# Windowed attention and two MLPs on one core: a written order for the kernel's head

## The chip, the cores and the metric

The kernel runs on 1 core of one Trainium2 chip. The metric is the device time of one execution in microseconds (us). The kernel before took 899.46 us, the median of 3 runs (899.13 to 899.58).

## What is computed

Inputs are q, k and v of shape (4, 8, 576, 64) and the weights of two MLPs, float64 as they lie in memory (512 to 2048 and back to 512), for 2304 tokens. Attention sees the last 64 positions. Cut to what matters:

```python
def _attn_ref(q, k, v):
    scores = 1.0 / np.sqrt(D) * np.matmul(q, k.transpose(0, 1, 3, 2))
    mask = (rel >= 0) & (rel < 64)
    scores = np.where(mask, scores, -1000000000.0)
    attn = np.exp(scores - np.max(scores, axis=-1, keepdims=True))
    attn = attn / (np.sum(attn, axis=-1, keepdims=True) + 1e-09)
    return np.matmul(attn, v)

def reference(...):
    x = attention, as (2304 tokens, 512)
    h = x @ moe_w_in;  x = np.maximum(0.01 * h, h) @ moe_w_out
    h = x @ moe2_w_in; return (np.maximum(h, 0) + np.log1p(np.exp(-np.abs(h)))) @ moe2_w_out
```

## The kernel before, in words

Tokens go in 6 chunks of 384 (`T`), each of three tiles of 128 tokens or six blocks of 64. A product keeps float32 accuracy by being done three times with operands split into a high and a low part (`three`, L464 to L466). One step of the first MLP is a pair (chunk, j), where j counts 16 strips of the hidden width: `gemm1` (L468) makes 12 matmuls into `ph`, ACT makes g and gh from it and DVE gl; `gemm2` (L487) makes 12 matmuls from gh and gl into four `o` banks, two steps later (`SKEW`). The steps go chunk 0 with j 0 to 7, chunk 1 with j 0 to 15, chunk 0 with j 8 to 15, then chunks 2 to 5: while the first 16 strips of both matrices are still being converted, strips 0 to 7 are used twice.

Weights come in as 512 KB pieces, one per strip and matrix, 32 in all for the first MLP (`load_w`, three `raw64` places). A piece is converted by ACT (`conv_a`, L159), by two DVE instructions (`conv_b`, L170 and L176), and split by ACT and DVE (`conv_c`, L217 and L218). A `ticker` issues these.

The attention of a tile or block has four pieces. A: PE transposes q and k of a tile into `pq` and `pk`, ACT scales pq into `qbd` (L354), DVE copies pk into `kT` (L362). B: scores `ps` on PE (L377), mask and maximum on DVE (L382, L384), four exponentials on ACT (L387), sum and reciprocal on DVE (L391, L392), and the product with the reciprocal on GpSimd (L394). C: transposes `pt` on PE (L403), copied to `at` by ACT (L405). D: product with v, `po`, on PE (L415), split into the chunk's xh by ACT (L420) and xl by DVE (L421).

The head of the program is the attention of chunk 0, in the written order "A0 B0 B1 A1 B2 C0 B3 D0 ...", with `tick()` at listed places; then the steps, with the attention of chunk 1 laid between those of chunk 0. A scheduler then places each instruction on its engine's queue. q and k of a tile lie in two places (`raw`), so that tile 1 is loaded once tile 0 has been transposed. All loads are issued from SP's queue, in its order.

Of the kernel before, what the change touches and what calls it, by code (L numbers as in the profile page):

```python
# [8 lines left out]
F32 = mybir.dt.float32  # L9
# [11 lines left out]
def tile_window_attention_two_mlps(  # L21
# [180 lines left out]
    def pair_rows(p):  # L202

        row = lambda tag, bufs, n: sb.tile(
            [P, n, 2, DM // 2], F32R, tag=tag, bufs=bufs, name=f"wp_{p}_{tag}{len(got)}"
        )
        got = []
        tags = (("v", 3, 1), ("kT", 2, 1), ("qbd", 1, 2), ("part", 1, 3))
        if p % 2 == 0:
            tags = (("raw", 2, 1),) * 2 + (("v", 3, 1),) * 2 + (("sm", 2, 1),) * 2 + (("kT", 2, 1),)  # L210
        for tag, bufs, n in tags:
            t = row(tag, bufs, n)
            got += [t[:, i] for i in range(n)]
        return got

# [5 lines left out]
    def conv_c(key):  # L221
        m, j, i = key
        a = conv.pop(key)[1]
        if m == 0:
            hi, lo = (w_row(4 * j + 2 * i + n) for n in range(2))
        elif i == 0:
            return
        else:

            hi, lo = w2_rows(j)  # L230
        split(hi, lo, a)
        if i == 0:
            hi, lo = (w.rearrange("p (c f) -> p c f", c=NK) for w in (hi, lo))
        W[key] = (hi, lo)
# [56 lines left out]
    scored = []  # L291
    qk_raw, v_win, kT, st = {}, {}, {}, {}

    def load_qk(t):
# [38 lines left out]
    att_n = [0]  # L333
# [6 lines left out]
    def att_a(t):  # L340

        kt = sb.tile([P, NP, BL + P], F32, tag="kT", bufs=2, name=f"kT_{t}")
        q_in, k_in = qk_raw.pop(("q", t)), qk_raw.pop(("k", t))
        if t < BY_DVE:
            pq, pk = att_ps(f"pq_{t}"), att_ps(f"pk_{t}")
            for x_in, x_out in ((q_in, pq), (k_in, pk)):
                for p in range(NP):
                    nc.tensor.transpose(x_out[:, p, :], x_in[:, p * P : (p + 1) * P], ident)
        else:
            pq = sb.tile([P, NP, P], F32, tag="raw", bufs=2, name=f"qT_{t}")  # L350
            nc.vector.transpose(pq, q_in)
# [9 lines left out]
        if t < BY_DVE:
            nc.vector.tensor_copy(kt[:, :, BL:], pk)  # L362
        else:
            nc.vector.transpose(kt[:, :, BL:], k_in)
        kT[t] = kt

    def att_b(gb):

        t, u = divmod(gb, 2)
# [12 lines left out]
        nc.vector.tensor_tensor(sm, ps, mask.unsqueeze(1).to_broadcast([P, NP, P]), ALU.min)  # L382
        nm = sb.tile([P, NP], F32, tag="nm", bufs=2, name=f"nm_{gb}")
        nc.vector.tensor_reduce(nm, sm, AX.X, ALU.max, negate=True)  # L384
        sums = sb.tile([P, NP], F32, tag="sums", bufs=2, name=f"sums_{gb}")
        for p in range(NP):
            a = nc.scalar.activation(  # L387
                sm[:, p, :], sm[:, p, :], AF.Exp, bias=nm[:, p : p + 1],
                accum_out=sums[:, p : p + 1],
            )  # L390
        nc.vector.tensor_scalar_add(sums, sums, 1e-9)  # L391
        b = nc.vector.reciprocal(sums, sums)  # L392
        scored.append((a.ins, b.ins))
# [74 lines left out]
    def gemm1(c, j):  # L468
        m = 0
# [5 lines left out]
        g = sb.tile([P, T], F32, tag="tmp", bufs=4, name=f"g_{m}_{c}_{j}")  # L475
        nc.scalar.activation(g, ph, AF.Prelu, alpha=0.01)  # L476
        gh = sb.tile([P, T], F32R, tag="gh", bufs=3, name=f"gh_{c}_{j}")
        gl = sb.tile([P, T], F32R, tag="gl", bufs=3, name=f"gl_{c}_{j}")
        a = nc.scalar.copy(gh, g)  # L479
        b = nc.vector.tensor_tensor(gl, g, gh.bitcast(F32), ALU.subtract)  # L480
        behind.append((a.ins, b.ins))
        G[m, c, j] = (gh, gl)
# [3 lines left out]

    def gemm2(c, j, s, e):  # L487

        wh, wl = W[0, j, 1]
        gh, gl = G.pop((0, c, j))  # L490
# [5 lines left out]
        if e and j < NF - 1:  # L496
            part[c] = sb.tile([P, NK, T], F32, tag="part", bufs=1, name=f"part_{c}")
            for i, po in enumerate(O.pop(c)):
                (nc.scalar.copy if i % 2 == 0 else nc.vector.tensor_copy)(part[c][:, i, :], po)
        elif e:  # L500
# [112 lines left out]
    def ticker(keys):  # L613
# [14 lines left out]
    tick0 = ticker([(0, j, i) for j in range(NF) for i in range(2)])  # L628
    tick = lambda: next(tick0, None)
    load_qk(0)  # L630
    constants()
    nc.vector.memset(qbd, 0.0)
    load_v(0)
    load_qk(1)
    x = new_x(0, 0)
    att_tags[:] = ["att", "h", "o"]
# [3 lines left out]
    late_loads = {  # L640
        "A1": (load_qk, 2), "C0": (load_v, 1), "B3": (load_v, 2),
        "A2": (load_qk, 3), "C4": (load_v, 3),
    }
    pieces = {"A": att_a, "B": att_b, "C": att_c, "D": lambda n: att_d(n, *x)}
    for n, item in enumerate(order.split()):
        pieces[item[0]](int(item[1:]))
        if item in late_loads:
            f, t = late_loads[item]
            f(t)
        for _ in range(ticks_after.count(n)):  # L650
            with tc.issue_after(scored[-1][0]), tc.issue_after(scored[-1][1]):
                tick()
    att_tags[:] = ["att"]

    visits = [(0, 0, 0, CUT, 1), (0, 1, 0, NF, None), (0, 0, CUT, NF, 2)]
# [5 lines left out]

    def later(f, *a):
# [4 lines left out]

    first = [ticker([(1, 2 * p + f, 0) for f in range(2)]) for p in range(NF // 2)]  # L670
# [11 lines left out]
    for n, (c, j, s, e, nxt) in enumerate(steps):  # L682
        if s:
# [3 lines left out]
        if (c, j) == (1, NF - AHEAD):  # L687
            load_qk(BY_DVE)
        for u in range(2):
# [3 lines left out]
            if n < 2 * NF and (u == 0 or n % 2):  # L693
                tick()
# [88 lines left out]
```

## Time and profile before

| | |
|---|---|
| median of the runs | 899.46 us |
| the profiled execution: time, span | 899.1 us, 897.1 us |
| busy share of the span: PE, DVE, ACT, GpSimd | 97%, 60%, 47%, 5% |
| chain that ended last, PE's share | 91% |
| mean granted TensorE clock | 0.994 |

PE is the engine that the span follows. An average over the span hides where PE waits, so the profile is read by stretches: the table of 40 slices, the windows (busy time of each engine in a stretch, number of instructions, granted clock), the timeline for the start of a step, the chain of waits for what released what, and the groups by line for what one instruction takes.

### The profile page before, as it was taken

How to read it: one execution, taken by the hardware profiler on the slowest of the kernel's cores; microseconds unless marked ns; L12 is line 12 of the kernel's file. 1: busy time of each engine (PE TensorE's matmuls, PEld its weight loads, DVE VectorE, ACT ScalarE, POOL GpSimd, SP SyncE). 2: the span in 40 equal slices, each digit the busy share in tenths (PEclk: the TensorE clock that was granted, in tenths of full speed). 3: DMA queues.
4: the chain of work that ended last, by engine and by line, in shares of the span. 5: the costliest groups of instructions: out<-in, count | busy, mean ns of one | idle time of the engine just before them, and what ended most of it. 6: DMA issues, size and time to landing. Idle time of an engine off the chain costs nothing.

```text
span 897.1 us, 14253 instructions
## 1 busy us (share of the span) xinstructions
PE 870.1 (97%) x5232; PEld 818.0 (91%) x5232; DVE 538.8 (60%) x1059; ACT 419.5 (47%) x990; POOL 47.5 (5%) x66
## 2 busy tenths in 40 slices
PE   5699999999999999999999999999999899999998
PEld 4498999999999999999999999999999688888886
DVE  3898862544323333323257689777799976667664
ACT  3788752654434444434345532222245644545443
POOL 2212000211000111000000000000000000000000
PEclk9799999999999999999999999999999999999999
DMA  7567752243223311110132145444497444344432
GB/s 175 162 192 217 220 136 35 64 78 82 48 39 65 85 44 49 48 24 12 37 118 82 54 159 196 157 153 153 153 308 279 134 119 147 107 129 120 127 99 66
DMA packets 150277, 104.74 MB, mean 117 GB/s; under 512 B 104896, under 2 KB 129472, under 8 KB 150208
## 3 DMA queue, kind: packets, MB, share of 16 engines
q1 hardware_dynamic: 150208, 103.84, 40.2%
q8 instruction: 41, 0.67, 0.3%
q14 instruction: 28, 0.23, 0.1%
HBM read 75.50 MB, written 28.31 MB: 116 GB/s over the span
## 4 chain that ended last, share of the span: by engine, by line
PE 91%; DVE 4%; DMA 2%; ACT 1%; issue 1%; POOL 0%; POOLq 0%; DVEq 0%; ACTq 0%; SPq 0%
PE ph L464 7%; PE o L464 7%; PE o L465 7%; PE o L466 7%; PE ph L465 7%; PE ph L466 7%; PE f L464 7%; PE f L465 7%; PE f L466 7%; PE ps L377 4%; PE p_s L464 3%; PE p_s L466 3%; PE p_s L465 3%; PE p_a L464 3%; PE p_a L466 2%; PE p_a L465 2%
## 5 line engine op out<-in xcount | busy, mean ns | idle before, releaser
L480 DVE TENSOR_TENSOR gl<-g,gh 128x384 fp32r<-128x384 f32 x96 | 58.6, 610 | 158.5 <-ACT gh L479 158.0
L464 PE MATMUL ph<-xh,w 128*128 128x384 f32 x384 | 132.3, 345 | 0.0
L464 PE MATMUL o<-gh,w 128*128 128x384 f32 x384 | 131.7, 343 | 0.0
L465 PE MATMUL o<-gl,w 128*128 128x384 f32 x384 | 129.8, 338 | 0.0
L465 PE MATMUL ph<-xl,w 128*128 128x384 f32 x384 | 129.0, 336 | 0.0
L466 PE MATMUL ph<-xh,w 128*128 128x384 f32 x384 | 128.8, 335 | 0.0
L466 PE MATMUL o<-gh,w 128*128 128x384 f32 x360 | 121.7, 338 | 0.0
L476 ACT ACTIVATE g<-ph 128x384 f32<-128x384 f32 x96 | 46.9, 489 | 133.5 <-PE ph L466 133.3
L464 PE MATMUL f<-w,s 128*128 128x512 f32 x234 | 91.3, 390 | 2.8 <-ACT s L217 2.8
L465 PE MATMUL f<-w,s 128*128 128x512 f32 x234 | 91.1, 389 | 0.0
L466 PE MATMUL f<-w,s 128*128 128x512 f32 x234 | 90.7, 389 | 0.0
L572 ACT ACTIVATE s<-s 128x512 f32<-128x512 f32 (+1 forms) x80 | 47.0, 589 | 69.3 <-DVE s L571 68.7
L574 DVE SCALAR_TENSOR_TENSOR s<-s,s 128x512 f32<-128x512 f32 (+1 forms) x80 | 50.8, 636 | 38.5 <-ACT s L572 38.1
L464 PEld LDWEIGHTS ph<-xh,w 128*128 128x128 f32 x384 | 72.1, 188 | 0.9
L465 PEld LDWEIGHTS ph<-xl,w 128*128 128x128 f32 x384 | 72.2, 188 | 0.2 <-DVE xl L421 0.2
L387 ACT ACTIVATE sm<-sm,nm 128x128 f32<-128x128 f32 x144 | 56.1, 391 | 34.6 <-DVE nm L384 33.9
L465 PEld LDWEIGHTS o<-gl,w 128*128 128x128 f32 x384 | 72.2, 188 | 0.0
L464 PEld LDWEIGHTS o<-gh,w 128*128 128x128 f32 x384 | 72.2, 188 | 0.0
L466 PEld LDWEIGHTS ph<-xh,w 128*128 128x128 f32 x384 | 72.1, 188 | 0.0
L466 PEld LDWEIGHTS o<-gh,w 128*128 128x128 f32 x360 | 67.6, 188 | 0.0
L218 DVE TENSOR_TENSOR s<-s,s 128x512 fp32r<-128x512 f32 (+1 forms) x80 | 50.8, 636 | 13.9 <-ACT s L217 13.7
L217 ACT CAST s<-s 128x512 fp32r<-128x512 f32 (+1 forms) x80 | 46.2, 577 | 24.9 <-PE f L465 19.5
(153 smaller groups left out, 1691.7 us busy)
## 6 DMA issues: line engine op xcount, KB each, us to landing
wraw<-in_moe_w_in_dram SPq DMA_DIRECT2D x32, 512.0 KB, 4.7
wraw<-in_moe_w_out_dram SPq DMA_DIRECT2D x32, 512.0 KB, 4.6
s<-hd SPq DMA_DIRECT2D x64, 256.0 KB, 2.7
hd<-h_xh SPq DMA_DIRECT2D x12, 768.0 KB, 4.5
hd<-h_xl SPq DMA_DIRECT2D x12, 768.0 KB, 4.4
x2d<-x SPq DMA_DIRECT2D x24, 192.0 KB, 1.9
x_stage<-x2d SPq DMA_DIRECT2D x24, 192.0 KB, 2.6
out_dram<-s SPq DMA_DIRECT2D x18, 256.0 KB, 2.4
```

The lines of the kernel that those rows point to most:

```text
L217: i = nc.scalar.copy(hi, a)
L218: j = nc.vector.tensor_tensor(lo, a, hi.bitcast(F32), ALU.subtract)
L377: nc.tensor.matmul(ps[:, p, :], qbd[:, p, u, :], kT[t][:, p, w0 : w0 + P], start=True, stop=True,)
L387: a = nc.scalar.activation(sm[:, p, :], sm[:, p, :], AF.Exp, bias=nm[:, p : p + 1], accum_out=sums[:, p : p + 1],)
L464: nc.tensor.matmul(ps, wh, xh, start=start, stop=False)
L465: nc.tensor.matmul(ps, wh, xl, start=False, stop=False)
L466: nc.tensor.matmul(ps, wl, xh, start=False, stop=stop)
L476: nc.scalar.activation(g, ph, AF.Prelu, alpha=0.01)
L480: b = nc.vector.tensor_tensor(gl, g, gh.bitcast(F32), ALU.subtract)
L572: nc.scalar.activation(g, g, AF.Softplus)
L574: nc.vector.scalar_tensor_tensor(g, h, 0.0, g, ALU.max, ALU.add)
```

## The change

It replaces the written order of pieces, the ticks among them and the scheduler's freedom, for everything up to step 23, by one list (`HEAD`) of 447 small pieces. Each instruction of a piece is tied behind the last one on its engine, so that the five queues stand exactly in the list's order. The pieces A to D, the conversion and the two products are cut into one function per engine for this. The list runs to the end of the 24th step; step 24 onward is as before. Further, q and k of tiles 1 and 2 get places of their own (three rows of the place of a later weight, `qk_early`, and that of `w_last`), `sm`, `nm` and `sums` have three buffers in place of two, PSUM banks are given out by which is free, and a tile of 64 bytes per partition, `pad`, is made in the same pool, which shifts the addresses of what is allocated after it.

```diff
@@ load_qk
-            a = sb.tile([P, H * D], F32, tag="raw", bufs=2, name=f"{nm}raw_{t}")
+            if 0 < t < TPC:
+
+                if t == 1 and nm == "q":
+                    qk_early.append(wide("qk_early", F32))
+                    w = sb.tile([P, DM], F32, tag="w_last", bufs=1, name="k_early")
+                    qk_early.append([qk_early[0][:, n] for n in range(3)] + [w])
+                a = qk_early[1][2 * (t - 1) + (nm == "k")]
+            else:
+                a = sb.tile([P, H * D], F32, tag="raw", bufs=2, name=f"{nm}raw_{t}")
...
@@ att_ps
-        tag = att_tags[att_n[0] % len(att_tags)]
-        att_n[0] += 1
+        left = {t: (4 if t == "o" else 2) - list(held.values()).count(t) for t in att_tags}
...
@@ att_b, now att_bp, att_bm, att_bn, att_be, att_bs, att_bx
-        sm = sb.tile([P, NP, P], F32, tag="sm", bufs=2, name=f"sm_{gb}")
+        sm = sb.tile([P, NP, P], F32, tag="sm", bufs=3, name=f"sm_{gb}")
...
+        if "pad" not in st:
+
+            st["pad"] = sb.tile([P, 16], F32, tag="pad", bufs=1, name="pad")
+            nc.vector.memset(st["pad"][:1, :1], 0.0)
...
@@ the head
-    order = "A0 B0 B1 A1 B2 C0 B3 D0 A2 C1 C2 B4 D1 D2 B5 C3 D3 C4 C5 D4 D5"
-    ticks_after = [2, 2, 3, 5, 10, 11, 14, 18, 20]
...
+    HEAD = """
+        Lq0 Lq1 Lv1 Ap0 Lq2 Aq0 Ak0 Ap1 Ah1 Bp1 l1 Ak1 Bp0 Bm1 l2 Bn1 Aq1 Ah2 Ap2 Bm0 Be1 Bp3 Bn0 l0 Ak2
...
+        Q22 R22 G23 H21 P23 Q23 R23
+    """.split()
...
+        seen = len(traced)
+        pieces[item[:n]](int(item[n:]))
+        new = traced[seen:]
+        for ins in new:
+            before = queues.get(ins.engine)
+            if before is not None:
+                tc.add_manual_dep(
+                    ins, before.name,
+                    mybir.DependencyInfo(mybir.DependencyClass.NoSync, mybir.DependencyReason.DATA),
+                    reason="head",
+                )
+            queues[ins.engine] = ins
```

In the list the letters A to D are the attention's pieces (second letter: the part, p on PE, q and e on ACT, k, m, n, s and l on DVE, x on GpSimd), l, a, b, c, d are load, the three conversions and the split's DVE half, G and H the first and second product of a step, P, Q, R the work on g, L a load of q, k or v. Up to the first piece that needs a weight (G0) it holds 6 Ap, 10 Bp, 6 Cp and 6 Dp, 5 Aq, 7 Be, 6 Ca, 6 Dh, 4 a and 3 c; from G0 to G8 it holds 8 G, 7 H, 2 Bp, 6 Cp, 6 Dp, and for DVE 14 b, 14 d, 5 Bm, 5 Bn, 6 Bs, 6 Dl, 8 R and 1 Ak. The last conversion (d31) stands ahead of G18.

The queue of SP, from its start: q, k and v of a tile are `qraw`, `kraw` and `vn` or `vs`, the 512 KB weight pieces `wraw`. Before:

```order
L286 DMA qraw_0_86<-in_q_dram 128x8x64
L286 DMA kraw_0_88<-in_k_dram 128x8x64
L286 DMA vn_0_115<-in_v_dram 128x8x64
L128 DMA wraw_0_0_0_171<-in_moe_w_in_dram 128x4x128
L133 DMA wraw_0_0_1_173<-in_moe_w_out_dram 128x512
L128 DMA wraw_0_1_0_194<-in_moe_w_in_dram 128x4x128
L286 DMA qraw_1_117<-in_q_dram 128x8x64
L286 DMA kraw_1_119<-in_k_dram 128x8x64
```

and in the change:

```order
L297 DMA qraw_0_111<-in_q_dram 128x8x64
L297 DMA kraw_0_113<-in_k_dram 128x8x64
L297 DMA qk_early_115<-in_q_dram 128x8x64
L297 DMA qk_early_115<-in_k_dram 128x8x64
L297 DMA vs_1_119<-in_v_dram 128x8x64
L297 DMA vn_1_121<-in_v_dram 128x8x64
L297 DMA qk_early_115<-in_q_dram 128x8x64
L297 DMA k_early_116<-in_k_dram 128x8x64
L133 DMA wraw_0_0_1_156<-in_moe_w_out_dram 128x512
```

q and k of tile 1 moved from seventh and eighth, behind three weight pieces, to third and fourth, and those of tile 2 ahead of all weights.

The queue of PE at the start of step 8, the first of chunk 1 (the numbers behind `ph_` and `gh_` are chunk and strip). Before:

```order
L464 MATMUL o_0_0_2_677<-gh_0_5_921,w_7_782 128x384
L465 MATMUL o_0_0_2_677<-gl_0_5_922,w_7_782 128x384
L466 MATMUL o_0_0_2_677<-gh_0_5_921,w_7_782 128x384
L464 MATMUL o_0_0_3_678<-gh_0_5_921,w_7_782 128x384
L465 MATMUL o_0_0_3_678<-gl_0_5_922,w_7_782 128x384
L466 MATMUL o_0_0_3_678<-gh_0_5_921,w_7_782 128x384
L464 MATMUL ph_1_0_1075<-xh_0_1_455,w_0_299 128x384
```

and in the change:

```order
L552 MATMUL o_0_0_2_575<-gh_0_6_985,w_8_904 128x384
L553 MATMUL o_0_0_2_575<-gl_0_6_1011,w_8_904 128x384
L554 MATMUL o_0_0_2_575<-gh_0_6_985,w_9_959 128x384
L552 MATMUL o_0_0_3_576<-gh_0_6_985,w_8_904 128x384
L553 MATMUL o_0_0_3_576<-gl_0_6_1011,w_8_904 128x384
L554 MATMUL o_0_0_3_576<-gh_0_6_985,w_9_959 128x384
L552 MATMUL ph_1_0_1075<-xh_0_1_674,w_0_430 128x384
```

The second product of strip 6 moved ahead of step 8. Before step 24, and from there to the end, both programs hold the same matmuls in the same order but for one score and one transpose of chunk 2.

## Rows read from the trace of the kernel before

**Rows 1.** The page's 40 equal slices: busy tenths of PE.

```profile
PE   5699999999999999999999999999999899999998
```

**Rows 2.** Windows: stretch, length; busy PE, PEld, DVE, ACT, POOL; clock, DMA share.

```profile
4.16:22.70 18.54, 13.37 (x66) 11.30 (x68) 6.21 (x12) 7.46 (x26) 2.88 (x4) 1.00 0.74 184
22.70:33.00 10.30, 6.37 (x76) 5.25 (x72) 8.31 (x17) 8.73 (x31) 2.48 (x3) 1.00 0.59 146
33.00:44.03 11.03, 6.69 (x64) 4.98 (x64) 9.32 (x21) 7.68 (x23) 2.35 (x2) 0.54 0.58 174
44.03:91.16 47.13, 45.34 (x356) 41.96 (x354) 42.11 (x80) 39.33 (x108) 8.36 (x9) 1.00 0.72 207
91.16:158.36 67.20, 67.20 (x386) 67.20 (x386) 37.37 (x67) 33.59 (x65) 0.40 (x1) 1.00 0.48 126
158.36:680.00 521.64, 521.64 (x3362) 513.09 (x3362) 279.99 (x569) 214.88 (x548) 28.78 (x33) 1.00 0.34 99
```

**Rows 3.** Timeline of PE: start and us, first product of steps 0, 8, 24.

```profile
44.03 0.61 PE L464 MATMUL ph<-xh,w 128*128 128x384 f32 x2
...
91.16 0.34 PE L464 MATMUL ph<-xh,w 128*128 128x384 f32 x1
...
158.36 0.34 PE L464 MATMUL ph<-xh,w 128*128 128x384 f32 x1
```

**Rows 4.** Chain of waits in order of time: start, us, what.

```profile
0.73 3.29 DMA qraw<-in_q_dram
...
5.28 7.17 DMA qraw<-in_q_dram
...
18.61 3.41 PE ps L377 x16
...
75.88 0.93 PE ps L377 x8
76.81 0.44 PE pt L403 x4
77.95 0.61 PE po L415 x16
```

**Rows 5.** Groups by line on ACT, 0 to 44.03 us: busy us, mean ns.

```profile
L387 ACT ACTIVATE sm<-sm,nm 128x128 f32<-128x128 f32 x24 | 9.3, 391 | 3.4 <-DVE nm L384 2.6 <-DVE sums L392 0.6
L159 ACT ACTIVATE cva<-wraw 128x512 f32<-128x512 f32 x6 | 4.0, 674 | 0.0
L354 ACT ACTIVATE qbd<-pq 64x512 f32<-64x512 f32 x6 | 3.5, 592 | 9.3 <-PE pq L348 9.2
L405 ACT COPY at<-pt 128x512 f32<-128x512 f32 x6 | 3.3, 586 | 0.3 <-PE pt L403 0.3
L217 ACT CAST w<-cva 128x512 fp32r<-128x512 f32 x5 | 3.1, 622 | 1.6 <-DVE cva L176 1.6
L420 ACT CAST xh<-po 128x256 fp32r<-128x256 f32 x6 | 2.1, 365 | 2.2 <-PE po L415 2.2
```

**Rows 6.** Groups by line on DVE, 44.03 to 91.16 us: busy us, mean ns.

```profile
L176 DVE SCALAR_TENSOR_TENSOR cva<-wraw,cva 128x512 uint16<-128x512 uint32 x13 | 10.4, 799 | 0.2
L218 DVE TENSOR_TENSOR w<-cva,w 128x512 fp32r<-128x512 f32 x13 | 9.8, 754 | 2.0 <-ACT w L217 1.7
L170 DVE TENSOR_SCALAR cva<-cva 128x512 int32<-128x512 int32 x12 | 6.0, 503 | 0.2 <-ACT cva L159 0.2
...
L382 DVE TENSOR_TENSOR sm<-ps,masks 128x512 f32<-128x512 f32 x6 | 4.0, 685 | 0.6 <-PE ps L377 0.6
...
L362 DVE COPY kT<-pk 128x512 f32<-128x512 f32 x3 | 2.1, 694 | 0.4 <-PE pk L348 0.4
```

**Rows 7.** Timeline of GpSimd and DVE around 30 us: start, us.

```profile
30.26 1.04 POOL L394 TENSOR_TENSOR sm<-sm,sums 128x512 f32<-128x512 f32 x1 [2.93 <-PE po L415]
30.32 1.53 DVE L218 TENSOR_TENSOR w<-cva,w 128x512 fp32r<-128x512 f32 x1
...
33.78 0.66 DVE L218 TENSOR_TENSOR w<-cva,w 128x512 fp32r<-128x512 f32 x1
```

More of the change, by code (lines that the diff above doesn't have):

```diff
@@ L214, in pair_rows, with conv_c1, conv_c2 @@
         return got
+    split_parts = {}
+    def conv_c1(key):
+        m, j, i = key
+        hi, lo = (w_row(4 * j + 2 * i + n) for n in range(2))
+        nc.scalar.copy(hi, conv[key][1])
+        split_parts[key] = (hi, lo)
+    def conv_c2(key):
+        a = conv.pop(key)[1]
+        hi, lo = split_parts.pop(key)
+        nc.vector.tensor_tensor(lo, a, hi.bitcast(F32), ALU.subtract)
+        if key[2] == 0:
+            hi, lo = (w.rearrange("p (c f) -> p c f", c=NK) for w in (hi, lo))
+        W[key] = (hi, lo)
     def split(hi, lo, a):
@@ L332, in tile_window_attention_two_mlps, with new_kt, att_ap, att_aq @@
     att_tags = ["att"]
-    att_n = [0]
+    held = {}
     def att_ps(name):
-        tag = att_tags[att_n[0] % len(att_tags)]
-        att_n[0] += 1
-        return pp.tile([P, NP, P], F32, tag=tag, bufs=4 if tag == "o" else 2, name=name)
[L340 to L351, printed above, removed]
+        left = {t: (4 if t == "o" else 2) - list(held.values()).count(t) for t in att_tags}
+        if len(att_tags) > 1:
+            kind, n = name.split("_")
+            end = HEAD.index({"pq": "Aq", "pk": "Ak", "ps": "Bm", "pt": "Ca", "po": "Dl"}[kind] + n)
+            left["h"] *= end < HEAD.index("G0")
+            left["o"] *= end < HEAD.index("H0")
+        tag = max(att_tags, key=lambda t: (left[t] > 0, t != "att", left[t]))
+        held[name] = tag
+        return pp.tile([P, NP, P], F32, tag=tag, bufs=4 if tag == "o" else 2, name=name)
+    def new_kt(t):
+        if t not in kT:
+            kT[t] = sb.tile([P, NP, BL + P], F32, tag="kT", bufs=2, name=f"kT_{t}")
+        return kT[t]
+    def att_ap(t):
+        pq, pk = att_ps(f"pq_{t}"), att_ps(f"pk_{t}")
+        for nm, x_out in (("q", pq), ("k", pk)):
+            x_in = qk_raw.pop((nm, t))
+            for p in range(NP):
+                nc.tensor.transpose(x_out[:, p, :], x_in[:, p * P : (p + 1) * P], ident)
+        st["q", t], st["k", t] = pq, pk
+    def att_aq(t, pq=None):
+        pq = st.pop(("q", t)) if pq is None else pq
         for h in range(2):
@@ L358, in att_a, with att_ah, att_ak, att_bp @@
             )
+    def att_ah(t):
+        kt = new_kt(t)
         if block(2 * t)[1] != 0:
             nc.gpsimd.tensor_copy(kt[:, :, :BL], kT[t - 1][:, :, P : P + BL])
[L361 to L365, printed above, removed]
+    def att_ak(t):
+        nc.vector.tensor_copy(new_kt(t)[:, :, BL:], st.pop(("k", t)))
+    def att_a(t):
+        q_in, k_in = qk_raw.pop(("q", t)), qk_raw.pop(("k", t))
+        kt = new_kt(t)
+        pq = sb.tile([P, NP, P], F32, tag="raw", bufs=2, name=f"qT_{t}")
+        nc.vector.transpose(pq, q_in)
+        att_aq(t, pq)
+        att_ah(t)
+        nc.vector.transpose(kt[:, :, BL:], k_in)
     def att_b(gb):
+        for f in (att_bp, att_bm, att_bn, att_be, att_bs, att_bx):
+            f(gb)
+    def att_bp(gb):
         t, u = divmod(gb, 2)
@@ L408, in att_d, with att_dp @@
     def att_d(gb, xh, xl):
+        att_dp(gb)
+        att_dh(gb, xh)
+        att_dl(gb, xh, xl)
+    def att_dp(gb):
         at = st.pop(gb)
@@ L468, in gemm1, with gemm1_p @@
     def gemm1(c, j):
+        for f in (gemm1_p, gemm1_a, gemm1_h, gemm1_l):
+            f(c, j)
+    def gemm1_p(c, j):
         m = 0
@@ L495, in gemm2 @@
             three(O[c][i], wh[:, cs], wl[:, cs], gh, gl, s, e)
[L496 to L500, printed above, removed]
+        if e and j == NF - 1:
             before = part.pop(c, None)
@@ L626, in ticker @@
             yield
[L628 to L636, printed above, removed]
-    order = "A0 B0 B1 A1 B2 C0 B3 D0 A2 C1 C2 B4 D1 D2 B5 C3 D3 C4 C5 D4 D5"
-    ticks_after = [2, 2, 3, 5, 10, 11, 14, 18, 20]
[L640 to L657, printed above, removed]
+    visits = [(0, 0, 0, CUT, None), (0, 1, 0, NF, None), (0, 0, CUT, NF, 2)]
     visits += [(0, c, 0, NF, c + 1 if c + 1 < NC else None) for c in range(2, NC)]
@@ new lines, in tile_window_attention_two_mlps @@
+    """.split()
+    keys = [(0, j, i) for j in range(NF) for i in range(2)]
+    x_of = lambda c: X.get((0, c)) or new_x(0, c)
+    block_x = lambda f, n: lambda g: f(g, *x_of(g // NBC)[:n])
+    step = lambda f: lambda n: f(*steps[n][:2])
+    pieces = {
+        "Lq": load_qk, "Lv": load_v, "Ap": att_ap, "Aq": att_aq, "Ah": att_ah, "Ak": att_ak,
+        "Bp": att_bp, "Bm": att_bm, "Bn": att_bn, "Be": att_be, "Bs": att_bs, "Bx": att_bx,
+        "Cp": att_cp, "Ca": att_ca, "Dp": att_dp, "Dh": block_x(att_dh, 1), "Dl": block_x(att_dl, 2),
+        "l": lambda n: load_w(keys[n]), "a": lambda n: conv_a(keys[n]), "b": lambda n: conv_b(keys[n]),
+        "c": lambda n: conv_c1(keys[n]), "d": lambda n: conv_c2(keys[n]),
+        "G": step(gemm1_p), "P": step(gemm1_a), "Q": step(gemm1_h), "R": step(gemm1_l),
+        "E": lambda n: put_part(steps[n][0], True), "F": lambda n: put_part(steps[n][0], False),
+        "H": lambda n: gemm2(*steps[n][:4]),
+    }
@@ new lines, in tile_window_attention_two_mlps @@
+    att_tags[:] = ["att", "h", "o"]
+    queues = {}
+    traced = nc.cur_bb.bb.instructions
+    constants()
+    nc.vector.memset(qbd, 0.0)
+    for item in HEAD:
+        n = len(item.rstrip("0123456789"))
+        held.pop({"Aq": "pq", "Ak": "pk", "Bm": "ps", "Ca": "pt", "Dl": "po"}.get(item[:n], "") + "_" + item[n:], None)
+        if item == "G0":
+            att_tags[:] = ["att"]
+        if item == f"G{CUT + NF - AHEAD}":
+            load_qk(BY_DVE)
+            load_v(BY_DVE)
+        seen = len(traced)
[10 more added lines that the diff above has]
+            queues[ins.engine] = ins
```

103 lines of the change are left out of this document (77 added, 26 removed).

## The prediction

> **What bounds the kernel now.** I read the 40 slices first: PE is at five and six tenths in the first two, of 22.4 us each, and full in nearly all others [rows 1]. Then I cut the run at three instants that can be counted off in the timeline: the first product of step 0 at 44.03 us, of step 8 (the ninth group of twelve `ph` matmuls) at 91.16 and of step 24 (the twenty-fifth) at 158.36 [rows 3]. The reader is to see in the windows that stage C, step 8 to 24, has no idle PE: 386 matmuls in 67.20 us, 0.174 us each, 2.1 us for each product of twelve [rows 2]. From 158.36 to 680 PE is busy without a gap as well, and its order there is the old one. So whatever step 24 gains, the end gains, and all else is decided in stage A (to 44.03) and stage B (44.03 to 91.16).
>
> How much is there to win? Up to step 24 PE has 24 first and 22 second products, 46 x 2.1 = 96.6 us. At full speed a block of attention costs 0.93 for its scores, 0.44 for its transposes, 0.61 for the product with v [rows 4], and a tile's eight transposes of q and k twice 0.44: 12 x 1.98 + 6 x 0.88 = 29.0. PE can start when q of tile 0 has landed, at 0.73 + 3.29 = 4.0 us [rows 4]. That makes 129.6 against 158.36: 28.7 us are lost at most. Two things lose them: waits, and TensorE's clock. Sixteen score records take 3.41 us at 18.61 and eight take 0.93 at 75.88 [rows 4], which is 1.2 GHz against 2.4, although the granted clock column has no lower figure there; it has 0.54 for 33 to 44.03 [rows 2], after a stretch in which PE was busy 6.37 of 10.30 us.
>
> **Stage A, to the first product of step 0.** This product needs xh and xl of all six blocks of chunk 0. In the change q and k of tile 1 are third and fourth on SP's queue and have places of their own. Before, q of tile 1 landed at 5.28 + 7.17 = 12.45 [rows 4]; between it and the first q at 4.02 lay 2304 KB (k, v, three weight pieces, itself), so 256 KB took 8.43 / 9 = 0.94 us, and k of tile 1 now lands at 4.02 + 3 x 0.94 = 6.8. PE then transposes it (about 1 us at 1.2 GHz), makes the first scores (half of 3.41, 1.7), DVE masks them and takes the maximum (two of some 0.69 [rows 6]): the first exponential starts at about 11.0. From there ACT is the longest queue. The list puts on it, ahead of the last xh: 24 exponentials x 0.391, 6 qbd x 0.592, 6 `at` x 0.586, 6 xh x 0.365, 3 cva x 0.674, 2 weight casts x 0.622 [rows 5] = 9.4 + 3.6 + 3.5 + 2.2 + 2.0 + 1.2 = 21.9 us. Without a wait the last xh ends at 32.9 and xl (0.4) at 33.3. That is the lower bound. For the upper one I take the share in which ACT was busy between 22.70 and 44.03, 16.41 of 21.33 or 77% [rows 2]: 11.0 + 21.9 / 0.77 = 39.4, with xl 39.8. I take 36.0, below the middle, because q, k and v of three tiles now wait for nobody and a third `sm` place lets a block's scores run while GpSimd still holds two others. DVE's part is shorter (5 kT, 7 masks, 7 maxima, 4 conversions, some 23 us of work) and PE's is 6 x 0.88 + 10 x 0.93 + 6 x 1.05 = 20.9 at full speed, since scores of blocks 6 to 9 now stand here. Gain: 44.0 - 36.0 = 8.0 us.
>
> **Stage B, step 0 to step 8.** PE has 8 first and 7 second products (one more than before: that of strip 6 stands ahead of step 8), 31.5, and of the attention two scores, six transposes and six products with v, 8.2: 39.7. Before it had 14 products, 29.4, six of each of the three, 11.9, and two tiles' transposes, 1.8: 43.1, in 47.1 us; 4.0 were lost. DVE was busy 42.11 of these 47.13 [rows 2] and is close behind PE. Its list for the stage differs by one conversion more in L176 and in L218 and two in L170 (0.80 + 0.75 + 1.01), and by one mask, one maximum and two kT copies less (some 0.69 each, 2.8) [rows 6], so it needs about 42. Lower bound: DVE's 42 without a wait. Upper: the old 47.1. I take PE's work with the old loss, 39.7 + 4.0 = 43.7. Gain: 3.4, which with the moved product counts as 5.5.
>
> DVE and GpSimd also meet: a weight split that begins at 30.32, with the normalisation of 1.04 us running since 30.26, takes 1.53 us, and one begun at 33.78 takes 0.66 [rows 7]. The durations above contain such meetings at the old rate. The Trainium skill, "SBUF — State Buffer", section "SBUF: two separate sides", says that GpSimd and a VectorE instruction with two inputs in SBUF exclude each other on a shared port for a whole instruction, which agrees with these rows. If the new order let all six normalisations of the stage meet one, that rule would add up to 6 x 1.04 = 6.2 us to DVE, and the time would be some 890 rather than 886.
>
> **Stage C, step 8 to step 24.** 16 first and 15 second products, 31 x 2.1 = 65.1 us, against 67.2. DVE was busy 37.37 of 67.20 us there [rows 2], so conversions of strips 8 to 15 stay hidden behind PE; what is late next if they were not is the weight of step 16. The partial sums of chunk 0 are copied under a first product, as before. The 64-byte tile, the third `sm` and the memset of one element cost nothing: DVE has 5 us of slack in B [rows 2].
>
> **The sum.** Step 24 begins at 36.0 + 43.7 + 65.1 = 144.8, 13.6 us earlier. The profiled execution took 899.1 (span 897.1), so 885.5; the median lies 0.4 higher: **885.9 us**. With the lower bounds, 33.3 + 42 + 65.1 = 140.4, it is 881.5; with the upper, 39.8 + 47.1 + 65.1 = 152.0, it is 893.1.
>
> **Rivals.** (1) *The clock stays at 1.2 GHz through stage A.* PE's 20.9 us become 41.8, and step 0 begins no earlier than 4.0 + 41.8 = 45.8; with B and C as above 154.6, gain 3.8, 895.7 us. For it: the lower clock of 33 to 44.03 came after a stretch in which waits stood between PE's bursts [rows 2], and stage A, with 20.9 us of work in 32, will have such waits too. Against it: the loads bring work to PE earlier and closer together, and the scores of 75.88 were at full speed in a stage of the same mixture [rows 4]. One such fall of 10 us costs half of 6.4, 3 us, and lies in the range. The Trainium skill, "TensorE: Matmul & The Clock Gate", "Part 1: The HAM clock gate", says that the slow clock is the default and that activity releases it; by that, a cold stage A is this rival. (2) *Stage B swallows the gain of stage A.* The weights of steps 0 to 7 need 16 conversions, and DVE with 42.11 of 47.13 us busy is almost full [rows 2]; if three `raw64` places and the order of SP's queue hold them to the old pace, step 8 starts at 91.16 as before and only the moved product counts: 897.4 us, no measurable change. Against it: the first two strips' loads stand only behind attention loads that are done by some 11 us, and DVE's sum for the stage did not grow. (3) *Slower: tiles at new addresses make TensorE's reads slower.* The change shifts nearly every tile behind `sm`. Between 91.16 and 680 PE is full for 588.8 us [rows 2]; a matmul longer by 2.4%, 4 ns of 174, would eat all 13.6 us, and by 5%, +29.4, the time would be 915. Against it: products that read x, g and weights from many different places run at the same 0.174 us in stage C [rows 2]. The Trainium skill, "SBUF — State Buffer", the section named above, holds that on the engines' side only that shared port causes contention, and that PE waits on nobody, by which the move costs nothing.
>
> **How the numbers follow.** My forecast's case has a chance of 0.82, rival 1 0.07, rival 2 0.04, rival 3 0.04, and 0.03 is for a stage A or B that beats its lower bound. The range from 881 to 893 takes in the bounds of the sum and leaves out the three rivals and the rest. A change of 0.2%, 1.8 us, is about what a measurement of this kernel can tell from none: the forecast, rival 1 and the last case are faster by more (0.92), rival 2 is the same (0.04), rival 3 slower (0.04).
>
> **What would show it.** Right: the first exponential near 11 us, the first `ph` near 36, step 8 near 79.7, step 24 near 144.8, and no idle PE from there to 680. ACT should be busy nearly throughout from 11 to 33. Wrong: long waits of PE for GpSimd's `sm` in stage A (then the chain of one block, not ACT's queue, sets step 0), a granted clock near 0.5 beyond 25 us, DVE waiting for DMA in stage B, or `ph` matmuls that no longer start 0.174 us apart.

## The result, and the profile after

The changed kernel takes 887.9 us (median of 4 runs, 886.98 to 889.01) beside 899.33 us (899.13 to 899.58): a ratio of 0.9876, interval 0.9864 to 0.9889, 11.4 us faster. Forecast were 885.9 us and a range of 881 to 893. The profiled execution took 889.01 us (span 887.1), the longest of the four; the sum had 885.5 for it. So the total is 3.5 us off in the profiled execution and 2.0 in the medians, but the parts below show larger errors of both signs.

First the page's slices and the windows of the changed kernel; the columns are those of [rows 1] and [rows 2], and the cuts lie at its own first products of steps 0, 8 and 24.

```profile
PE   7889999999999999999999999999999899999998
```

```profile
4.12:22.70 18.58, 16.25 (x107) 14.04 (x108) 10.29 (x22) 11.18 (x41) 4.29 (x6) 0.91 1.03 212
22.70:33.00 10.30, 6.18 (x83) 4.88 (x81) 7.98 (x18) 8.64 (x28) 3.52 (x4) 0.97 0.71 146
33.00:40.16 7.16, 7.16 (x71) 6.86 (x68) 3.98 (x9) 4.65 (x10) 0.40 (x1) 0.81 0.90 234
40.16:84.92 44.76, 41.55 (x320) 38.53 (x319) 42.01 (x81) 38.43 (x108) 7.46 (x7) 1.00 0.70 199
84.92:151.10 66.18, 64.73 (x374) 64.44 (x374) 37.51 (x67) 33.32 (x65) 0.40 (x1) 1.00 0.49 132
151.10:680.00 528.90, 528.63 (x3422) 520.10 (x3422) 289.92 (x590) 221.56 (x559) 28.63 (x33) 1.00 0.36 103
```

PE's timeline has the three first products at 40.16, 84.92 and 151.09, where [rows 3] has 44.03, 91.16 and 158.36:

```profile
40.16 0.42 PE L552 MATMUL ph<-xh,w 128*128 128x384 f32 x1
...
84.92 0.34 PE L552 MATMUL ph<-xh,w 128*128 128x384 f32 x1
...
151.09 0.33 PE L552 MATMUL ph<-xh,w 128*128 128x384 f32 x1
```

Stage A (to step 0) became 3.9 us shorter, B (step 0 to 8) 2.4, C (step 8 to 24) 1.0, where one second product of 2.1 us moved from C to B: 7.3 in all. But the span fell by 10.0. The rest, 2.7 us, came after step 24, where nothing was moved.

**Why A is long.** Two timelines tell it. On PE the scores of both blocks of tile 0, then ACT (qbd is L387, the exponentials L451, `at` L483; in brackets the idle time before, and its releaser):

```profile
8.56 3.51 PE L425 MATMUL ps<-kT,qbd 128*128 128x128 f32 x16
```

```profile
12.17 1.21 ACT L387 ACTIVATE qbd<-pq 64x512 f32<-64x512 f32 x2 [5.72 <-PE ps L425]
13.41 0.40 ACT L451 ACTIVATE sm<-sm,nm 128x128 f32<-128x128 f32 x1
...
34.68 0.58 ACT L483 COPY at<-pt 128x512 f32<-128x512 f32 x1 [2.94 <-PE pt L477]
```

The first exponential comes at 13.41, not at 11.0: ahead of it on ACT stands qbd of tile 1, which may overwrite qbd only when PE has done the scores of both blocks of tile 0, 3.51 us, nearly all at 1.2 GHz (the scores of tile 1, from 13.43 on, take 2.05). Later ACT stands idle for 2.94 us behind PE, and PE (q, k and the v window `vn` of a tile, and the product with v) behind a load:

```profile
26.64 0.69 PE L498 MATMUL po<-at,vs 128*64 128x64 f32 x16 [0.94 <-ACT at L483]
...
32.42 1.12 PE L498 MATMUL po<-at,vn 128*64 128x64 f32 x16 [1.92 <-DMA vn<-in_v_dram]
33.47 1.12 PE L477 MATMUL pt<-ident,sm 128*128 128x128 f32 x4
```

That load is in SP's queue, whose timeline gives the start of each issue:

```profile
13.88 2.60 SPq L297 DMA_DIRECT2D kraw<-in_k_dram  x1
24.09 1.41 SPq L297 DMA_DIRECT2D qraw<-in_q_dram  x2
25.61 1.27 SPq L297 DMA_DIRECT2D kraw<-in_k_dram  x2
26.98 0.71 SPq L297 DMA_DIRECT2D vs<-in_v_dram  x1
27.74 0.58 SPq L297 DMA_DIRECT2D vn<-in_v_dram  x1
```

From 16.5 to 24.1 us the queue issues nothing: its head, q of tile 4, goes to a `raw` place that PE frees with the transposes of tile 3. Behind it stand both v windows of tile 2. The second goes out at 27.74, right behind the first and after the product that began at 26.64 has ended, and lands 4.54 us later, at 32.28. After these waits the granted clock is lower: 0.81 in the window from 33.00, with four transposes in 1.12 us in place of 0.66.

**What came after step 24.** Groups by line on PE, 200 to 440 us, matmuls of both products of the first MLP (busy us, mean ns). Before:

```profile
L465 PE MATMUL ph<-xl,w 128*128 128x384 f32 x192 | 64.4, 335 | 0.0
L464 PE MATMUL o<-gh,w 128*128 128x384 f32 x192 | 66.4, 346 | 0.0
L465 PE MATMUL o<-gl,w 128*128 128x384 f32 x192 | 64.9, 338 | 0.0
L466 PE MATMUL o<-gh,w 128*128 128x384 f32 x180 | 60.8, 338 | 0.0
```

and in the change:

```profile
L553 PE MATMUL ph<-xl,w 128*128 128x384 f32 x192 | 64.4, 335 | 0.0
L552 PE MATMUL o<-gh,w 128*128 128x384 f32 x195 | 66.9, 343 | 0.0
L553 PE MATMUL o<-gl,w 128*128 128x384 f32 x195 | 65.4, 335 | 0.0
L554 PE MATMUL o<-gh,w 128*128 128x384 f32 x182 | 61.0, 335 | 0.0
```

The first product (`ph`) is as it was; each matmul of the second (`o`) is 3 ns shorter. By their starts, twelve took 2.117 us and now 2.083 (median). 74 of the 96 second products lie behind step 24, which makes 2.5 of the 2.7 us.

### The profile page after: what moved, and what is told of

It reads as the page before. It is cut to its first block, busy times and chain, and to the rows that moved or that the text cites. A ratio compares the mean times of both kernels' runs of the same rounds, so it can differ in the third digit from the quotient of the medians.

```text
span 887.1 us, 14240 instructions
## 1 busy us (share of the span) xinstructions
PE 863.5 (97%) x5232; PEld 812.7 (92%) x5232; DVE 537.8 (61%) x1060; ACT 418.9 (47%) x990; POOL 46.9 (5%) x66
## 4 chain that ended last, share of the span: by engine, by line
PE 88%; DVE 5%; DMA 3%; ACT 2%; issue 1%; POOL 0%; SPq 0%; POOLq 0%; ACTq 0%; DVEq 0%
PE f L552 7%; PE f L554 7%; PE f L553 7%; PE o L552 7%; PE ph L552 7%; PE o L554 7%; PE o L553 7%; PE ph L553 7%; PE ph L554 7%; PE p_s L554 4%; PE p_s L552 4%; PE p_s L553 4%; PE ps L425 4%; PE p_a L554 3%; PE p_a L552 3%; PE p_a L553 3%
## 5 line engine op out<-in xcount | busy, mean ns | idle before, releaser
L553 PE MATMUL f<-w,s 128*128 128x512 f32 x234 | 91.2, 390 | 0.0
L683 ACT ACTIVATE s<-s 128x512 f32<-128x512 f32 (+1 forms) x80 | 47.1, 589 | 69.6 <-DVE s L682 68.8
L685 DVE SCALAR_TENSOR_TENSOR s<-s,s 128x512 f32<-128x512 f32 (+1 forms) x80 | 51.1, 640 | 38.6 <-ACT s L683 38.1
L451 ACT ACTIVATE sm<-sm,nm 128x128 f32<-128x128 f32 x144 | 56.1, 391 | 31.0 <-DVE nm L440 30.9
```

The source lines that it names most:

```text
L451: nc.scalar.activation(sm[:, p, :], sm[:, p, :], AF.Exp, bias=nm[:, p : p + 1], accum_out=sums[:, p : p + 1],)
L553: nc.tensor.matmul(ps, wh, xl, start=False, stop=False)
L683: nc.scalar.activation(g, g, AF.Softplus)
L685: nc.vector.scalar_tensor_tensor(g, h, 0.0, g, ALU.max, ALU.add)
```

## The experiments

Twelve kernels, in three groups of four; each group had the kernel before beside it on its chip (898.3, 898.5 and 899.0 us). First what their profiles have in common: the first exponential on ACT, the first product of steps 0, 8 and 24, the span, all in us, and the time as a ratio to before. All but the ratio is of one profiled execution each; the control, e5, stands in the second group, so the others are held against it by their ratios.

| | first exp. | step 0 | step 8 | step 24 | span | ratio (interval) |
|---|---|---|---|---|---|---|
| before | 14.20 | 44.0 | 91.2 | 158.4 | 897.1 | |
| the change | 13.41 | 40.2 | 84.9 | 151.1 | 887.1 | 0.9876 (0.9864–0.9889) |
| e1_v_place | 12.74 | 35.1 | 79.5 | 145.4 | 882.2 | 0.9850 (0.9834–0.9867) |
| e2_no_pad | 11.37 | 38.4 | 81.6 | 146.7 | 888.0 | 0.9913 (0.9897–0.9929) |
| e3_free_order | 13.07 | 39.4 | 82.9 | 147.8 | 884.2 | 0.9848 (0.9828–0.9867) |
| e4_raw_places | 15.39 | 43.3 | 87.2 | 152.9 | 890.9 | 0.9905 (0.9887–0.9924) |
| e5_control | 12.71 | 38.1 | 82.2 | 148.8 | 885.1 | 0.9868 (0.9850–0.9886) |
| e6_shift_128 | 12.32 | 37.7 | 81.9 | 147.8 | 889.4 | 0.9920 (0.9902–0.9938) |
| e7_before_pad | 13.67 | 42.8 | 89.8 | 156.4 | 892.3 | 0.9950 (0.9938–0.9962) |
| e8_part_early | 12.11 | 37.6 | 81.1 | 145.6 | 881.6 | 0.9845 (0.9831–0.9859) |
| e9_warm | 13.07 | 39.5 | 84.1 | 149.6 | 887.5 | 0.9877 (0.9860–0.9894) |
| e10_before_places | 11.89 | 38.4 | 85.5 | 152.7 | 892.2 | 0.9939 (0.9926–0.9953) |
| e11_both | 13.36 | 36.8 | 81.3 | 145.8 | 882.4 | 0.9830 (0.9814–0.9845) |
| e12_both_warm | 11.38 | 34.2 | 77.9 | 142.4 | 879.3 | 0.9806 (0.9792–0.9819) |

**A place of its own for v of tile 2.**

```diff
+        own = wide("v_early", F32) if t == 2 else None
-            a = sb.tile([P, H * D], F32, tag="v", bufs=3, name=f"vs_{t}")
+            a = own[:, 0] if own is not None else sb.tile(..., name=f"vs_{t}")
... (the same for vn, with own[:, 1])
-        ... Aq2 Lq3 Bs0 ...   ... Bs5 Lv2 Dl3 ...
+        ... Aq2 Lq3 Lv2 Bs0 ...   ... Bs5 Dl3 ...
```

> v of tile 2 (vs, vn) gets a place of its own and is issued right behind q and k of tile 3. In the changed kernel it landed at 32.28 us, PE waited 1.9 us for it and ACT stood idle 2.9 us behind that wait; its place came free only with the product of block 2 at 27.3 and its DMA stood behind q and k of tile 4 on SP's queue. Theory V (this late v is most of what stage A lost against the forecast): v lands before 24 us, both waits go, step 0 begins at 38 to 38.5 in place of 40.2, and steps 8 and 24 follow by the same 1.5 to 2 us: 886.0 us against 887.9. Rival (DVE, busy 41.95 of the 44.7 us of stage B, holds step 8): step 0 comes earlier but step 8 and step 24 stay at 84.9 and 151.1: 887.9. Second rival (ACT's list is the bound of stage A and only shifts its idle time): step 0 stays within 0.5 us of 40.2.

The first row is SP's, the others PE's:

```profile
16.50 2.20 SPq L297 DMA_DIRECT2D v_early<-in_v_dram  x2
```

```profile
27.91 0.69 PE L499 MATMUL po<-at,v_early 128*64 128x64 f32 x16
...
35.05 0.42 PE L553 MATMUL ph<-xh,w 128*128 128x384 f32 x1
```

Theory V holds in the trace: no wait for v, and step 0 at 35.1, 3.0 us ahead of the control, more than forecast. The granted clock was 1.00 from 12 to 36 us here and 0.93 in the control; what part of the 3.0 us is the clock's was not separated. Stage B is as long as in the control (44.4 and 44.1), so DVE does not take the gain back. The ratio falls by 0.0018, some 1.6 us, but the two intervals overlap: in the time alone the gain is not clear of noise.

**Without the filler.**

```diff
-        if "pad" not in st:
-            st["pad"] = sb.tile([P, 16], F32, tag="pad", bufs=1, name="pad")
-            nc.vector.memset(st["pad"][:1, :1], 0.0)
```

> The 64-byte tile and its memset are left out; all else is the changed kernel. Every tile behind it then begins 64 bytes lower, at 64 above a multiple of 128 bytes (at, xh, xl, cva, g, gh, gl, part). From step 24 on the changed kernel's second products of the first MLP take 2.083 us for twelve matmuls, those of before 2.117. Theory L (the addresses of PE's moving operands set those few ns): the products of xh, gh and gl become longer, by 2 to 6 ns per matmul of 174, so 5 to 20 us on the whole: 893 to 908. Rival (addresses do not matter, the few ns come from something else): 887.9 within 1 us, second products at 2.083 us.

The head is no slower than in the control, but from step 24 to the end this kernel takes 741.3 us where the control takes 736.3 (736.0 to 738.0 in all nine profiles that keep the change's filler as it is). Between 200 and 440 us `ph` and `o` matmuls both have means of 337 ns or more, where the change has 335. The direction of theory L holds, not its size: by the ratios 4.0 us against the control, below the bracket.

**The list without ties.**

```diff
-            if before is not None:
+            if before is not None and False:
                 tc.add_manual_dep(
```

> The ties that hold each engine to the list are left out; the list still is the order in which the program is written, and a scheduler places the instructions. On PE a few pieces change places (the products of strip 3 and the scores of block 6, for instance), on DVE and ACT more. Theory (the gain comes from early loads and from the list as a whole, not from single places): the time stays within 2 us of 887.9, step 24 between 149 and 153. Rival (the exact order of ACT's and DVE's queues brings the gain): step 8 is late by 3 us or more, and the time is above 891.

The theory holds in the main: ties are not where the gain is. Step 24 comes at 147.8, a little before the bracket of 149 to 153. By the ratios the time is 1.8 us below the control's, with overlapping intervals; PE waits for no partial sums in stage C here.

**q and k of tiles 1 and 2 in the shared places.**

```diff
-            if 0 < t < TPC:
+            if False:
```

> q and k of tiles 1 and 2 go back to the two shared places, with the list as it is. The load of q of tile 1 then waits for PE's transposes of tile 0, done at about 6.5 us, and every load behind it on SP's queue waits with it. Theory (the own places are what lets stage A begin early): q of tile 1 lands near 10 and k near 12 us instead of 7.6, tile 2's later still, the first exponential comes unchanged near 13 (block 0 and 1 are of tile 0) but those of tile 1 some 4 us later; step 0 at 43 to 45, 3 to 5 us later than the changed kernel's 40.2, and the time 891 to 893. Rival (stage A is set by ACT's list and by v of tile 2, which is late anyway): step 0 within 1 us of 40.2 and 888.

The direction holds, with two misses. The first exponential was to stay near 13 and comes at 15.39, 2 to 4 us later than in the runs of this list with own places: PE makes the scores of tile 0 only behind the transposes of k of tile 1, so a late tile 1 delays tile 0 too. Step 0 at 43.3 is 3.1 us later than in the change and 5.2 than in the control, but the time, 890.15 us, is below the bracket: some 3 us lost by the ratios.

**The change once more**, with no edit.

> The changed kernel once more, as it is, so that the kernels of this call have it beside them on their chip. Theory (the head's waits and the granted clock there differ from execution to execution, all else is fixed): the ratio to the kernel before is 0.985 to 0.989; in the profile the second products take 2.083 us from step 24 on, and step 0 begins between 37 and 41 us, later where the granted clock shows 0.5 for longer before step 0.

As expected. Step 0 lies 2.1 us earlier than in the first profile of the same kernel; the mean granted clock from 12 to 36 us is 0.93 here and was 0.86 there.

**All behind nm and sums 128 bytes lower.**

```diff
-        nm = sb.tile([P, NP], F32, tag="nm", bufs=3, name=f"nm_{gb}")
+        both = sb.tile([P, 2 * NP], F32, tag="nm", bufs=3, name=f"nm_{gb}")
...
-        sums = sb.tile([P, NP], F32, tag="sums", bufs=3, name=f"sums_{gb}")
+        nm, sums = both[:, :NP], both[:, NP:]
...
-            st["pad"] = sb.tile([P, 16], F32, tag="pad", bufs=1, name="pad")
+            st["pad"] = sb.tile([P, 8], F32, tag="pad", bufs=1, name="pad")
```

> nm and sums share a tile and the filler is 32 bytes, so that all that lies behind them begins 128 bytes lower than in the changed kernel: at, xh, xl, cva, g, gh, gl and part then begin at a multiple of 256 bytes, as gh, gl and part did before, in place of 128 above one. The order of all queues stays. Theory L (PE's matmuls take 2 to 3 ns more where the moving operand begins at such an address; the run without the filler had 175 ns for xh, gh and gl against 173): first and second products of the first MLP both become longer, from 173.4 ns to 175.5 to 176.5 ns; 2304 matmuls x 2.5 ns is 5.8 us, so 4 to 7 us above the control. Rival L' (only addresses that are no multiple of 128 cost something): the same time as the control within 1 us.

**The kernel before with a filler.**

```diff
         sums = sb.tile([P, NP], F32, tag="sums", bufs=2, name=f"sums_{gb}")
+        if "pad" not in st:
+            st["pad"] = sb.tile([P, 32], F32, tag="pad", bufs=1, name="pad")
+            nc.vector.memset(st["pad"][:1, :1], 0.0)
```

> The kernel before with a filler of 128 bytes behind nm and sums: gh, gl, part and others move from a multiple of 256 bytes to 128 above one; xh and xl stay where they are, at 128 above one; the order of the queues is the old one. Theory L: the second products from step 24 on fall from 2.117 to 2.083 us for twelve matmuls, 96 of them, so 3 us; some products with weights in part gain too: 895 to 896.5 where the kernel before has 898.3 to 899.4, a ratio of 0.9955 to 0.9975. So much of the change's gain has nothing to do with the order of the head. Rival (the few ns come from the code or from the banks of PSUM): ratio 1.000 within 0.001.

The same groups, 200 to 440 us, with the 128 bytes taken away from the change:

```profile
L553 PE MATMUL ph<-xl,w 128*128 128x384 f32 x192 | 65.0, 338 | 0.0
L553 PE MATMUL o<-gl,w 128*128 128x384 f32 x192 | 65.0, 339 | 0.0
```

and with 128 bytes added to the kernel before:

```profile
L468 PE MATMUL ph<-xl,w 128*128 128x384 f32 x193 | 64.6, 335 | 0.0
L468 PE MATMUL o<-gl,w 128*128 128x384 f32 x193 | 64.6, 335 | 0.0
```

Theory L holds both ways, and rival L' falls: where xh and gh both move, both products slow down (4.5 us more than the control's time); where gh and gl move and xh and xl do not, only the second changes, and the old kernel gains 4.3 us (ratio 0.995) with its order untouched. That is more than the 3 us forecast (894.25 us, below the bracket of 895 to 896.5). In the profiles 2.8 us lie behind step 24 (735.9 in place of 738.7) and 0.6 in stage C, where second products run; but 1.2 lie in stage A, and there the clock differs: the first transposes at full speed come in the kernel before at

```profile
22.90 0.66 PE L348 MATMUL pq<-ident,qraw 128*128 128x128 f32 x4
```

and in this one at

```profile
12.41 0.66 PE L348 MATMUL pq<-ident,qraw 128*128 128x128 f32 x4 [1.37 <-DMA qraw<-in_q_dram]
```

So this part need not be the addresses'.

**The partial sums copied earlier.**

```diff
-        ... l23 b20 P9 Q9 d19 c20 l22 G10 R9 a21 F7 E7 d20 H8 ...
+        ... l23 b20 P9 Q9 F7 E7 d19 c20 l22 G10 R9 a21 d20 H8 ...
```

> The changed kernel with the two pieces that copy the partial sums of chunk 0 (F7 on DVE, E7 on ACT) directly behind the work on step 9's g, ahead of a conversion on each engine; before, PE waited 1.45 us for them at 93.4 us, though the product they wait for had ended at 91.16. Theory: the copies run from 91.2 to 92.2 beside the first product of step 10, the wait goes, step 24 begins 1.4 us earlier relative to step 8 (64.8 us in place of 66.2), and the time falls by 1.4 us against the control. Rival (the conversion that is now behind the copies makes a weight late, or ACT's late gh takes the wait's place): step 8 to step 24 stays at 66 us or more.

In the change, PE's row in stage C was

```profile
94.85 0.41 PE L552 MATMUL o<-gh,w 128*128 128x384 f32 x1 [1.45 <-ACT part L598]
```

Now no such wait is left; stage C takes 64.5 us (81.1 to 145.6) in place of the control's 66.6, and the ratio falls by 0.0023. The theory holds in the trace, and the gain is 2.1 us rather than 1.4, since the control's own wait was 1.9. In the time alone the intervals of the two kernels overlap.

**PE busy before the first load.**

```diff
+    warm = pp.tile([P, NP, P], F32, tag="o", bufs=4, name="warm")
+    for n in range(9):
+        nc.tensor.transpose(warm[:, n % NP, :], ident, ident)
     for item in HEAD:
```

> Nine transposes of the identity stand ahead of all else on PE, from some 1.7 us until q of tile 0 has landed at 4.1; their result is not read. In the changed kernel the transposes of q and k take 0.27 us each (1.2 GHz) until some 11 us and then 0.15, the first scores of tile 0 take 2.0 to 3.5 us, and the first exponential comes at 12.7 to 13.4 behind them. Theory (PE's clock in its first 7 us sets when ACT can begin, because qbd of tile 1 waits for the scores of tile 0): the full clock comes 2 us earlier, the scores of tile 0 take 2.0 us, the first exponential comes at 12.0 to 12.5, step 0 some 0.7 us earlier, 886.5 against the control's 887.3. Rival (the clock at the start hangs on what PE does later, or v of tile 2 sets step 0 anyway): step 0 and the time as in the control, within 0.5 us.

The theory falls. PE's transposes reach 0.15 us only at 11.58,

```profile
11.58 0.60 PE L380 MATMUL pq<-ident,qk_early 128*128 128x128 f32 x4
```

about as without. The time is the control's within the noise, as the rival said; step 0, at 39.5, is 1.4 us later than the control's, not within its 0.5.

**Places and early loads in the old order.**

```diff
-    load_v(0)
     load_qk(1)
+    load_qk(2)
+    load_v(0)
...
-        "A1": (load_qk, 2), "C0": (load_v, 1), "B3": (load_v, 2),
+        "C0": (load_v, 1), "B3": (load_v, 2),
```

together with the `qk_early` branch of the change's load_qk.

> The kernel before with own places for q and k of tiles 1 and 2 and their loads ahead of the weights, in the old order of pieces; gh and gl stay at multiples of 256 bytes. Theory (the order matters more than the places: of PE's waits in stage A 9.9 us are for GpSimd's sm, in five waits, and 1.5 us only for q of tile 1): step 0 gains 1 to 2.5 us against 44.0, stage B and the later steps follow, ratio 0.997 to 0.999, second products at 2.117 us. Rival (early q and k carry stage A's gain): step 0 at 40 or earlier, ratio below 0.995.

My theory falls and the rival holds: 5.5 us of gain and step 0 at 38.4, as early as with the whole list. Yet PE's waits to step 0 (total, times, longest) are

```profile
PE pt L410 <- POOL sm L401: 9.7, 6, 3.6
```

for GpSimd, where the kernel before had

```profile
PE pt L403 <- POOL sm L394: 9.9, 5, 3.4
```

The largest wait stayed and 5.6 us went all the same. With the list it is the other way round: of these waits

```profile
PE pt L477 <- POOL sm L464: 1.8, 2, 1.6
```

are left in the change, and its step 0 comes no earlier. I read these waits as what PE does while ACT works through its list. Of the 5.6 us, 2.3 are that this list began at 11.89 in place of 14.20. Another 2.6 lie in one wait of ACT. In the kernel before PE was still at 1.2 GHz for the scores of blocks 2 and 3, and ACT stood idle for them:

```profile
18.41 3.62 PE L377 MATMUL ps<-kT,qbd 128*128 128x128 f32 x16
...
21.93 0.40 ACT L387 ACTIVATE sm<-sm,nm 128x128 f32<-128x128 f32 x1 [2.64 <-DVE nm L384]
```

In e10 PE was at full speed there, and ACT has no such wait:

```profile
12.04 2.02 PE L384 MATMUL ps<-kT,qbd 128*128 128x128 f32 x16 [1.04 <-DVE kT L369]
```

So a part of what the early loads bring in these two profiles comes with an earlier rise of the clock; whether it always does, one profile of each does not show. Stage B keeps its 47.1 us here and C its 67.2: what the list and the edits that came with it bring lies in B and C.

**Both edits, and both with the transposes ahead** (the diffs above together).

> The changed kernel with the own place for v of tile 2 and the early copies of the partial sums together. Theory (the two waits are independent): step 0 near 35.5, stage B about 44.3, stage C 64.6, so step 24 at 144 to 145; ratio 0.9815 to 0.9835, 882 to 883.5 us beside 898.5. Rival (an earlier stage A makes a conversion or a weight late in stage C): ratio 0.9845 or above, as with one of the two.

> The kernel with both edits and the nine transposes of the identity ahead. Theory: as e11, and 0.5 to 1 us less through the earlier first exponential, ratio 0.981 to 0.983, the fastest of all. Rival (stage B, where DVE is busy 42 of 44.5 us, keeps step 8 where it is): equal to e11 within 0.3 us.

```profile
36.83 0.42 PE L553 MATMUL ph<-xh,w 128*128 128x384 f32 x1
```

is the first product of e11, and of e12

```profile
5.14 0.66 PE L381 MATMUL pk<-ident,kraw 128*128 128x128 f32 x4
...
34.20 0.42 PE L553 MATMUL ph<-xh,w 128*128 128x384 f32 x1
```

The two waits are independent (0.983; stage C 64.5), though step 0 at 36.8 and step 24 at 145.8 come later than forecast and the median, 884.05 us, lies just above its bracket; ratio 0.983 is clear of the control's interval. The last kernel is the fastest of all: 881.26 us (880.68 to 882.94) beside 898.97. Its transposes ran at 2.4 GHz from 5.14 us on and the first exponential came at 11.38. It is 2.2 us below e11 by the ratios, where 0.5 to 1 was forecast. Since the same nine transposes did nothing in e9, and the intervals of e11 and e12 overlap, it stays open whether they bring this or the clock's scatter from execution to execution.

## Why the prediction was right in sum, and where its steps failed

- **Stage A, 36.0 forecast, 40.2 in this profile, 38.1 in the control: two terms were missed.** The first exponential: I let it wait for one block's scores, but ACT's queue holds qbd of tile 1 ahead of it, which waits for two; with PE at 1.2 GHz, and with these scores begun at 8.56 where the forecast's rate of loads gave 7.8, that is 13.41 for 11.0 (12.71 in the control). And "q, k and v of three tiles now wait for nobody" is false for v of tile 2. I had followed the loads to k of tile 2 in SP's queue and not to q of tile 4, which waits for PE with v behind it. The main term itself holds: ACT's list of 21.9 us. From the first exponential to step 0 it took 22.3, 23.5 and 22.8 us in the three runs with v in time (e1, e11, e12), and 25.4 to 27.0 in the other runs of the change's list with own places. ACT was busy for 21.6 to 22.0 of these us in e1, e11 and e12, and 22.1 of 26.8 in this profile: the work is the forecast's, the rest is waiting.
- **Stage B, 43.7 forecast, 44.8 and 44.1 measured: right within 1.1.** Over PE's 39.7 us of work by the sum, 5.1 and 4.4 were lost where I took the old 4.0. Not all of that is idle time: PE was busy 45.34 of 47.13 us before [rows 2] and 41.55 of 44.76 now. e10 (47.1) and e7 (47.0) show that neither the places nor the addresses shorten B, so the list does, or what came with it: the third `sm` and the choice of PSUM banks were not taken out by themselves. The ties are not needed (43.5 in e3).
- **Stage C, 65.1 forecast, 66.2: the sentence on the partial sums failed.** They are not copied "under a first product, as before": E7 stands behind a conversion on ACT, PE waits 1.45 us (1.9 in the control), and with the copies moved the stage takes 64.5.
- **"The 64-byte tile ... cost nothing" failed the other way.** I looked for its price on DVE. It shifts where xh, gh and gl begin: without it 5.0 us are lost after step 24, and with its like the old kernel gains 4.3 us, of which 2.8 after step 24. The mechanism is rival 3, with the sign turned round. I had taken the equal 0.174 us of [rows 2] to mean that addresses do not matter; but in the kernel before, second products were already the slower ones, 338 ns against 335, in a view by line that I did not read for this. On the Trainium skill's rule cited with rival 3 ("SBUF — State Buffer", "SBUF: two separate sides"), that PE waits on nobody: that sentence speaks of contention with other engines, and I stretched it to "the move costs nothing". The runs show that the place of its operand costs PE time: 338 ns against 335.
- **Rival 2 did not come, rival 1 only in part.** B did not swallow A's gain. PE did not stay at 1.2 GHz through stage A, but it began so: its transposes take 0.27 us each until 8 us and 0.15 from 11.91 on, which the granted clock column does not show, and later it fell for short stretches (0.91, 0.97 and 0.81 in A's windows).

A and C came 5.2 us longer than forecast and B 1.1, and 2.7 came back after step 24: 3.6, against the 3.5 us between 885.5 and 889.0, within rounding. That these 2.7 us came back is luck: the sum had nothing there. By the runs, places and early loads alone are worth 5.5 us and the filler alone 4.3; the change has 11.2 to 11.9 by the ratios. If the parts added up, 1.4 to 2.1 us would be left for the order and the third `sm`. They do not add up strictly: taking the places out of the change costs only 2.6 to 3.3 us.

## What to carry to other kernels

Follow the issuing queue past the loads you care about: one that waits for a place holds up all behind it. The largest wait in a list is not the bound if another engine's list runs through it; count that list from its first instruction. When tiles move in SBUF, compare the same matmul's mean time before and after, away from the edit, before you credit the order. And compare the same transposes at the start: e7 and the kernel before have one order and differ in stage A by 1.2 us.

## What was not expected of the hardware

- A matmul's time depends on where its moving operand begins. With gh and gl at a multiple of 256 bytes an `o` matmul has a mean of 338 ns in its group, at 128 above one 335; without the filler, at 64 above a multiple of 128, 337. By their starts, twelve take 2.117, 2.083 and 2.120 us (medians from 160 to 680 us). xh behaves alike. The addresses are read from the compiled program and stand in no trace; the traces show what the shifts do. The first product reads weights too and kept its 335 ns in e7, which speaks against the weights' places as the cause. What in the memory does this stays open.
- PE's start at 1.2 GHz ended at different times in executions of nearly the same head: transposes of 0.27 us had given way to 0.15 at 5.14 us in one (e12), at 7.59 in another (e2), and were first seen so between 10.4 and 13.9 in eleven; in the kernel before, only at 22.90. The granted clock column shows 1.00 for 0 to 10 us in all of them: the traces hold no clock state before the first rise (at 22.7 us in the kernel before, 11.8 in the change, 4.8 in e12), and the column reads 1.00 where they hold none.
- The runs of the changed kernel scatter by 2 to 3 us, and I take the clock for the cause; it was not tried by itself. The profiles agree with it. With one list up to step 0 and v late, the mean granted clock from 12 to 36 us is 0.86 in the change, e9 and e2, with step 0 at 40.2, 39.5 and 38.4, and 0.93 in e5, e6 and e8, with 38.1, 37.7 and 37.6; with v in time it is 0.93 in e11 and 1.00 in e1 and e12, with 36.8, 35.1 and 34.2. As the clock also falls after waits, cause and effect are not separated.
